# A recurrent attention layer with its gradients: order of the last forward block's stores, and one operand loaded in two halves

## The chip, the cores and the metric

The kernel runs on one core of a Trainium2 chip, as one program. Five engines work side by side, each through its own instructions in order: PE (TensorE, matrix products; its weight loads are listed apart as PEld), DVE (VectorE), ACT (ScalarE), POOL (GpSimd) and SP (SyncE, which here only issues DMAs). They wait for each other by semaphores. The metric is the device time of one execution in microseconds (us), median of several runs; lower is better.

## The reference

A sequence of 2048 rows of 512 numbers is normalised to `xn`. Output and all gradients are wanted of

```python
return x + _A_ref(xn, A_mem0, A_Wq, A_Wk, A_Wv, A_Wo, A_seg_len) + _B_ref(xn, B_w1, B_b1, B_w2, B_b2)
```

`_A_ref` goes through 64 segments of 32 rows, one after another. Each is attended together with 8 memory rows, 32 heads of 128, and the first 8 rows of its result are the next segment's memory:

```python
for s in range(n_seg):
    xs = x[:, s * seg_len:(s + 1) * seg_len, :].copy()
    h = jnp.concatenate([mem, xs], axis=1)
    q = jnp.einsum('btd,dhe->bhte', h, Wq)      # k, v alike
    ...
    p = _softmax(scores, axis=-1)
    o = jnp.einsum('bhqk,bhke->bhqe', p, v)
    o = jnp.einsum('bhte,hed->btd', o, Wo)
    mem = o[:, :M, :].copy()
    outs.append(o[:, M:, :])
```

`_B_ref` is a dense layer with bias, squared ReLU and a second dense layer (512 to 1792 to 512). `reference` calls `jax.vjp` and returns the output and ten gradients: of `x`, the first memory, Wq, Wk, Wv, Wo, w1, b1, w2, b2. The inputs are bf16.

## The kernel before

The work stands in five stages, in this order of time: the dense layer forward and backward (to about 240 us); the **forward chain** over 64 segments (to about 1125); the **left backward chain** (to about 1345); the backward chain over the segments, last to first; and the weight gradients as large products.

In the forward chain four segments make a block, 16 blocks in all. What depends only on the sequence itself, and not on the segment before, is the block's "left" part: the memory rows' own queries, keys and values. The order of all steps is written out by hand in the strings F_ORDER, one string for each of the four segments of a block. A name such as `q0mm+++` is a step of a segment, `L.lp` a step of a block's left part; each `+` delays it by one segment or block, and the strings are played for blocks 0 to 18, so that the last ones hold only what is left over. `play` calls each step once where its name stands.

Steps of a block's left part that the change touches, all of them DMAs on SP: `mtr` (L793) turns the memory rows' values vM into vTM, a tile with one buffer; `mst` (L794) stores it to S_VTM; `lp` (L844) stores the probabilities EL to S_PL; `otr` and `lo` (L841, L847) turn the left attention output OTL into ON and store it to S_OL; `lb` (L850) loads the dense result `bb`, to which DVE adds the block's output rows (L853). `t0` to `t3` and `u0` to `u3` turn and store the segments' attention output OT; for the last block, `t3` turns all four groups into one tile OCl and `u3` stores them (L782, L789), and then calls `st["late"]`, which is `otr` and `lo`. Other DMAs between them: `aw` and `as` (L946, L947) turn the dense layer's hidden gradients through a tile `box` to S_GH1N.

While the forward chain ends, PE also transposes the weights (ps_wt, copied back by ACT and DVE in turn), for the backward stages.

The left backward chain (`lback`, LB_ORDER) takes the 16 blocks in the order SEQ, beginning with 13, 14, 15. For each it needs the turned values l_vTL and l_vTM, the probabilities l_P and the keys l_kM and l_kL. The first block's loads, and the first dense chunk's, are issued by POOL (`first`), the later ones by SP (`ld`). Its PE work is interleaved with the dense weight gradients: each block carries one chunk of 256 hidden columns, `part` (wB, 1 MB, two buffers), against `side` (wA, 2 MB, all 2048 rows of the output gradient), written W0a, W0b, W1a, W1b. Blocks 1 to 7 make the gradient of w2 from `gflat` (each `a` half takes the first 8 of 16 row groups, each `b` half the others; L1106); blocks 9 to 15 make that of w1, with `side` loaded anew from S_XN (L1111). The chain's own stores (S_GOL, S_GSL, S_GQL) go out on POOL.

The tiles of the left backward chain lie in the SBUF space of the forward chain's tiles, so a first load waits until the last reader of what lay there is done, a DMA store among them. Names in the profile: tiles without buffer numbers, `S_...` for buffers in DRAM, `ps_...` for PSUM.

Of the kernel before, what the change touches and what calls it, by code (L numbers as in the profile page):

```python
# [10 lines left out]
BF16 = mybir.dt.bfloat16  # L11
F32 = mybir.dt.float32
P = 128
# [13 lines left out]
def kernel(  # L27
# [27 lines left out]
    nc = tc.nc  # L55

    _, S, D = A_x.shape
# [5 lines left out]
    L = M + SEG  # L63
# [3 lines left out]
    TC = S // P  # L67
# [21 lines left out]
    gflat = grad_out.flatten_outer_dims()  # L89
# [5 lines left out]
    dma = nc.sync.dma_start  # L95
    pdma = nc.gpsimd.dma_start
# [4 lines left out]
    NB = NSEG // SPB  # L101
# [12 lines left out]
    S_XN = dram.tile([S, D], BF16, name="S_XN")  # L114
# [6 lines left out]
    S_B = dram.tile([S, D], BF16, name="S_B")  # L121
# [9 lines left out]
    S_VTM = dram.tile([NB, P, KH, HG, NL], BF16, name="S_VTM")  # L131
    S_PL = dram.tile([NB, P, KH, KW], BF16, name="S_PL")
# [77 lines left out]
    with sb("p1b", 2) as p1b, sb("p1", 1) as p1:  # L210
# [90 lines left out]
        for rb in range(NRB):  # L301
# [5 lines left out]
            for fc in range(FC):  # L307
                ps = pst([P, RB], F32, name="ps_h1")
# [343 lines left out]
    def play(order, n, steps, lefts, step, blk, done=None):  # L652
# [37 lines left out]
        "tu1+++ w1+++ L.lq++ oa1+++ ob1+++ g0+++ g1+++ soN++ ra+++ rb+++ ta+++ Ha+++ tb+++ L.otr+ Hb+++ L.E3+ "  # L690
# [4 lines left out]
        "ta+++ Ha+++ rb+++ tb+++ Hb+++ km+++ L.t3+ q0mm++++ L.E5+ k0mm++++ L.ra+ xa+++ k0ev++++ q1mm++++ k1mm++++ "  # L695
# [5 lines left out]
    with psum("fr", 4) as fr, psum("fpp", 1) as fpp, \  # L701
# [58 lines left out]
        def left(b):  # L760
# [13 lines left out]
            for g in range(HG):  # L774
                def tO(g=g):
                    if b < NB - 1:
                        st["OC", g] = fo.tile([P, KH, P], BF16, name="OC", tag="OC", bufs=2)
                        nc.sync.dma_start_transpose(st["OC", g][:], B_["OT"][:, g].rearrange("p k j r -> p (k j r)"))
                    elif g == HG - 1:
                        st["OC"] = fs.tile([P, HG, KH, P], BF16, name="OCl", tag="OT")  # L780
                        for x in range(HG):
                            nc.sync.dma_start_transpose(st["OC"][:, x], B_["OT"][:, x].rearrange("p k j r -> p (k j r)"))  # L782

                def uO(g=g):
                    if b < NB - 1:
                        dma(S_ON[b, g], st["OC", g][:].rearrange("p k e -> p (k e)"))
                    elif g == HG - 1:
                        for x in range(HG):
                            dma(S_ON[b, x], st["OC"][:, x].rearrange("p k e -> p (k e)"))  # L789
                        st["late"]()  # L790
                o["t%d" % g], o["u%d" % g] = tO, uO

            o["mtr"] = lambda: nc.sync.dma_start_transpose(B_["vTM"][:].rearrange("p k g r -> p k (g r)"), B_["vM"][:])  # L793
            o["mst"] = lambda: dma(S_VTM[b], B_["vTM"][:])  # L794
            for p in range(2):
                def S_(p=p):
                    ps["s%d" % p] = big("ps_scL")
# [52 lines left out]
            o["lb"] = lambda: dma(B_["bb"][:], S_B[b * P:(b + 1) * P, :])  # L850

            def out():
                nc.vector.tensor_tensor(out=B_["bb"][:], in0=ps["B"][:], in1=B_["bb"][:], op=ALU.add)  # L853
# [140 lines left out]
    with sb("la", 2) as la, sb("ls", 2) as ls, sb("lo", 1) as lo_, sb("wg", 2) as wg, psum("lpp", 1) as lpp, psum("lr", 4) as lr:  # L994
# [8 lines left out]
        def lback(i_):  # L1003
# [10 lines left out]
            def load(i1, q=nc.sync):  # L1014
                T1, b1 = lb[i1][1], SEQ[i1]
                if i1:
                    turned_rows(T1["vTL"][:], b1, 2)
                q.dma_start(T1["vTM"][:], S_VTM[b1])
                q.dma_start(T1["P"][:], S_PL[b1])
                memory_rows(T1["kM"], b1, 2 * GW, q)  # L1020
                q.dma_start(T1["kL"][:], S_NL[b1][:, 1, :])

            def ld():
# [51 lines left out]
        NCH = F // CH  # L1075
        side, part = {}, {}

        def job(b):

            n, second = (b - 1, False) if b <= NCH else (b - NCH - 2, True)  # L1080
            return (n if 0 <= n < NCH else None), second

        def chunk(b, eng=dma):
            n, second = job(b)
            if n is None or b in part:
                return
            if n == 0:
                side[second] = wg.tile([P, TC, D], BF16, name="wA", tag="wA", bufs=1)
                pdma(side[second][:], (S_XN[:] if second else gflat).rearrange("(c p) f -> p c f", p=P))
            part[b] = wg.tile([P, TC, CH], BF16, name="wB", tag="wB")  # L1090
            eng(part[b][:], (S_GH1N if second else S_AN)[n])

# [4 lines left out]
        def product(b, i, x, ps):  # L1097
            n, second = job(b)
            if n is None:
                turns(2 if b == 0 else 5)  # L1100
                return
            if x == 0:
                ps["w", i] = big("ps_w")
            if not second:
                for rc in range(x * TC // 2, (x + 1) * TC // 2):
                    nc.tensor.matmul(ps["w", i][:], lhsT=part[b][:, rc, i * P:(i + 1) * P], rhs=side[False][:, rc, :],  # L1106
                                     start=(rc == 0), stop=(rc == TC - 1))
            else:
                dc = 2 * i + x
                for rc in range(TC):  # L1110
                    nc.tensor.matmul(ps["w", i][:, x * CH:(x + 1) * CH], lhsT=side[True][:, rc, dc * P:(dc + 1) * P],  # L1111
                                     rhs=part[b][:, rc, :], start=(rc == 0), stop=(rc == TC - 1), skip_group_check=True)
            if n == NCH - 1 and not second and i == 0 and x == 1:
                ps["b2"] = big("ps_gb2")
                for rc in range(TC):
                    nc.tensor.matmul(ps["b2"][0:1, :], lhsT=ones_col[:, :], rhs=side[False][:, rc, :], start=(rc == 0),
                                     stop=(rc == TC - 1))

        def keep(b, i, ps):
# [575 lines left out]
```

## Time and profile before

| | |
|---|---|
| median of 3 runs | 2846.58 us (2843.75 to 2865.32) |
| profiled execution | 2851.62 us, its span 2849.8 us |
| PE busy | 2660.2 us, 93% of the span |
| DVE, ACT, POOL busy | 1296.4, 976.6, 659.3 us |
| granted TensorE clock, mean | 0.979 |
| chain that ended last | PE 85%, issue 4%, DMA 4%, DVE 4%, SP's queue 2%, ACT 2% |
| DMA | 586.76 MB, mean 206 GB/s |

A row of the timeline reads: start in us from the span's start, busy us, engine, line, operation, result <- operands, form, number, and in brackets the idle time of that engine before it with what ended it. "SPq" is SP's DMA issuing; a DMA's row shows how long the issue took, not the transfer. A row of DMA issues ends with the median time from issue to landing. A row of waits says who waited for whom: us in total, times, longest. PE is the engine that sets the end almost everywhere, so a wait elsewhere counts only if PE comes to wait for it.

### The profile page before, as it was taken

How to read it: one execution, taken by the hardware profiler on the slowest of the kernel's cores; microseconds unless marked ns; L12 is line 12 of the kernel's file. 1: busy time of each engine (PE TensorE's matmuls, PEld its weight loads, DVE VectorE, ACT ScalarE, POOL GpSimd, SP SyncE). 2: the span in 40 equal slices, each digit the busy share in tenths (PEclk: the TensorE clock that was granted, in tenths of full speed). 3: DMA queues.
4: the chain of work that ended last, by engine and by line, in shares of the span. 5: the costliest groups of instructions: out<-in, count | busy, mean ns of one | idle time of the engine just before them, and what ended most of it. 6: DMA issues, size and time to landing. Idle time of an engine off the chain costs nothing.

```text
span 2849.8 us, 116970 instructions
## 1 busy us (share of the span) xinstructions
PE 2660.2 (93%) x52405; PEld 1452.3 (51%) x52405; DVE 1296.4 (45%) x3819; ACT 976.6 (34%) x2266; POOL 659.3 (23%) x1280
## 2 busy tenths in 40 slices
PE   7998999999999998888899899998999999999999
PEld 3444555555555556456455455555555544444444
DVE  4544656666666655344455555554555501100000
ACT  2323444444444445232333333333333301111111
POOL 1000000000000000123333433443334333322221
PEclk9999999999999999899999999999999999999999
DMA  9855689899989988998678877778777899999994
GB/s 248 273 193 179 162 190 216 214 214 220 219 208 220 222 207 184 268 244 229 157 186 175 205 189 175 181 198 205 175 178 192 236 337 199 210 221 206 212 205 84
DMA packets 840440, 586.76 MB, mean 206 GB/s; under 512 B 638001, under 2 KB 727746, under 8 KB 836610
## 3 DMA queue, kind: packets, MB, share of 16 engines
q1 hardware_dynamic: 798722, 455.76, 70.7%
q0 software_dynamic: 40928, 123.25, 14.9%
q8 instruction: 411, 6.73, 1.0%
q14 instruction: 91, 0.75, 0.1%
q10 hardware_dynamic: 288, 0.26, 0.0%
HBM read 184.95 MB, written 248.79 MB: 152 GB/s over the span
## 4 chain that ended last, share of the span: by engine, by line
PE 85%; issue 4%; DMA 4%; DVE 4%; SPq 2%; ACT 2%; POOL 0%; ACTq 0%; DVEq 0%; POOLq 0%
PE ps_gw L1653 19%; PE ps_proj L374 16%; PE ps_gR L492 12%; PE ps_R L492 5%; PE ps_RL L1260 3%; PE ps_tr L167 3%; PE b_pp L623 3%; PE ps_L L374 3%; PE ps_sc L464 2%; PE f_pp L623 2%; PE ps_B L345 2%; PE b_T L528 2%; PE ps_gxb L354 2%; PE f_T L528 2%; PE ps_w L1106 2%
## 5 line engine op out<-in xcount | busy, mean ns | idle before, releaser
L1653 PE MATMUL ps_gw<-gn,HNc 128*128 128x512 bf16 x1920 | 416.5, 379 | 0.0
L1653 PEld LDWEIGHTS <-HNc 128*128 128x128 bf16 x1920 | 187.9, 98 | 223.9
L419 ACT CAST f_N<-ps_proj 128x512 bf16<-128x512 f32 x320 | 184.0, 581 | 192.3 <-PE ps_proj L374 185.5
L1583 ACT CAST wt<-ps_gw 128x512 bf16<-128x512 f32 x128 | 73.7, 589 | 442.2 <-PE ps_gw L1653 410.4
L374 PEld LDWEIGHTS <-X 128*32 128x32 bf16 x5760 | 143.6, 96 | 134.0 <-DVE X L537 20.6
L1566 DVE TENSOR_TENSOR gx<-ps_rows,gb 128x512 f32<-128x512 f32 x16 | 11.1, 692 | 415.6 <-PE ps_rows L1564 415.6
L884 POOL COPY kM<-f_kT 128x256 bf16<-128x256 bf16 x64 | 25.8, 403 | 753.1 <-DVE f_kT L422 563.6
L492 PE MATMUL ps_gR<-Wv,gv 128*32 128x512 bf16 x2048 | 136.2, 390 | 6.0 <-issue 3.9
L1653 PE MATMUL ps_gw<-GOc,gn 128*128 128x512 bf16 x640 | 140.7, 382 | 1.2 <-DVE gm L1499 1.1
L492 PE MATMUL ps_R<-Wo,OT 128*32 128x256 bf16 x4096 | 131.6, 279 | 10.3 <-DMA Wo<-in_A_Wo_dram 4.5
L492 PE MATMUL ps_gR<-Wk,gk 128*32 128x512 bf16 (+1 forms) x2048 | 129.2, 375 | 3.6 <-issue 3.5
L374 PE MATMUL ps_proj<-Wo,GT 128*32 128x512 bf16 x2048 | 124.3, 384 | 5.7 <-DVE GT L1305 5.1
L1584 POOL DMA_DIRECT2D out_dram<-wt x120 | 65.0, 543 | 277.4 <-ACT wt L1583 260.5
L419 ACT CAST gON<-ps_proj 128x512 bf16<-128x512 f32 x128 | 75.0, 586 | 157.8 <-PE ps_proj L374 157.8
L374 PE MATMUL ps_proj<-Wq,X 128*32 128x512 bf16 x1920 | 126.0, 380 | 0.1
L492 PE MATMUL ps_gR<-Wq,gq 128*32 128x512 bf16 (+1 forms) x2048 | 120.3, 354 | 5.6 <-issue 5.6
L374 PE MATMUL ps_proj<-Wk,X 128*32 128x512 bf16 x1920 | 123.7, 382 | 0.6
L374 PE MATMUL ps_proj<-Wv,X 128*32 128x512 bf16 x1920 | 121.9, 378 | 0.2 <-issue 0.2
L1341 POOL COPY PD<-b_P 32x320 bf16<-32x320 bf16 x256 | 115.1, 450 | 14.9 <-DMA b_P<-S_A 3.7
L492 PEld LDWEIGHTS <-OT 128*32 128x32 bf16 x4096 | 105.6, 98 | 20.5 <-issue 13.5
L419 ACT CAST gk<-b_pp 128x256 bf16<-128x256 f32 x128 | 48.1, 376 | 166.6 <-PE b_pp L623 163.3
L492 PEld LDWEIGHTS <-gq 128*32 128x32 bf16 x2816 | 75.0, 98 | 56.2 <-issue 20.4
(291 smaller groups left out, 5278.8 us busy)
## 6 DMA issues: line engine op xcount, KB each, us to landing
S_A<-f_N SPq DMA_DIRECT2D x64, 512.0 KB
out_dram<-wt POOLq DMA_DIRECT2D x134, 128.0 KB, 5.5
S_A<-f_N SPq DMA_DIRECT2D x64, 256.0 KB
S_GB<-gv SPq DMA_DIRECT2D x32, 512.0 KB
S_GB<-gk SPq DMA_DIRECT2D x32, 512.0 KB
S_GB<-gq SPq DMA_DIRECT2D x32, 512.0 KB
b_qN<-S_A POOLq DMA_DIRECT2D x63, 256.0 KB, 4.3
b_kN<-S_A POOLq DMA_DIRECT2D x63, 256.0 KB, 5.2
```

Of the source, the lines that this page charges most:

```text
L167: nc.tensor.transpose(ps_ap, in_ap, ident[base:base + k, base:base + k])
L345: nc.tensor.matmul(psB[:], lhsT=aT[:, fc, rc * P:(rc + 1) * P], rhs=W2[:, fc, :], start=(fc == 0), stop=(fc == FC - 1))
L374: nc.tensor.matmul(o, lhsT=hT[:, dc, :], rhs=x, start=(dc == 0), stop=(dc == DC - 1), tile_position=(0, 32 * g))
L419: nc.scalar.copy(out, in_)
L492: nc.tensor.matmul(R[32 * g:32 * g + 32, 0:(cs.stop - cs.start) * P].rearrange("p (a b) -> p a b", b=P), lhsT=XT(k, g), rhs=x[:, cs, :], s ...
L528: nc.tensor.transpose(st["T", h][:, 0, c * P:(c + 1) * P], st["R4"][:, (2 * h + c) * P:(2 * h + c + 1) * P], identF[:])
L623: nc.tensor.matmul(o, lhsT=N_[32 * g:32 * g + m, kk * P:(kk + 1) * P], rhs=X(kk)[32 * g:32 * g + m], start=(i == 0), stop=(i == len(jobs) ...
L1260: nc.tensor.matmul(ps["R", i][32 * g:32 * g + 32, :].rearrange("p (a b) -> p a b", b=P), lhsT=B_[n][:, k, g, :], rhs=W(g * KH + k), start= ...
L1341: nc.gpsimd.tensor_copy(PD[32 * g:32 * g + 32, g], C["P"][32 * g:32 * g + 32, :, KW - L:KW])
L1583: nc.scalar.copy(wt[:], ps[:])
L1584: eng(dst, wt[:])
L1653: nc.tensor.matmul(ps[:], lhsT=l(rc), rhs=r(rc), start=(n == 0), stop=(n == RC_ALL - 1))
```

## The change

Three things. First, for the last block alone (`end = "z"`), the steps `mtr`, `lp`, `mst` and `lb` get names of their own, `mtrz`, `lpz`, `mstz` and `lbz`, which stand one or two strings earlier in F_ORDER than their plain names. Second, `otr` and `lo` of the last block are made where they are made for the others, and `late` goes. Third, `side` is two tiles of 8 row groups each, with a load for each; for the output gradient both are issued by POOL ahead of the first block's l_kL rather than behind it.

```diff
-        "k1ev+++ L.tu1+ q0fl+++ kl+++ xb++ L.mst k1fl+++ as- k0Te+++ soV++ q1ev+++ q0Te+++ L.W1+ q1fl+++ k1Te+++ "
-        "q1Te+++ L.hs+ L.oa1+ s0+++ mx0+++ sb0+++ L.X0+ v0mm+++ soP++ L.ob1+ s1+++ ex0+++ v1mm+++ su0+++ mx1+++ "
+        "k1ev+++ L.tu1+ q0fl+++ kl+++ xb++ L.mst L.mtrz+ k1fl+++ as- k0Te+++ soV++ q1ev+++ q0Te+++ L.W1+ L.lpz+ q1fl+++ k1Te+++ "
+        "q1Te+++ L.hs+ L.oa1+ s0+++ mx0+++ sb0+++ L.X0+ L.mstz+ v0mm+++ soP++ L.ob1+ s1+++ ex0+++ v1mm+++ su0+++ mx1+++ "
...
-        "kl+++ q0fl+++ as- xa++ q1ev+++ k0Te+++ k1fl+++ q1fl+++ q0Te+++ s0+++ L.ldL++ k1Te+++ mx0+++ q1Te+++ sb0+++ "
+        "kl+++ q0fl+++ as- xa++ L.lbz+ q1ev+++ k0Te+++ k1fl+++ q1fl+++ q0Te+++ s0+++ L.ldL++ k1Te+++ mx0+++ q1Te+++ sb0+++ "
...
-                        st["late"]()
...
+            end = "z" if b == NB - 1 else ""
+            o["mtr" + end] = lambda: nc.sync.dma_start_transpose(B_["vTM"][:].rearrange("p k g r -> p k (g r)"), B_["vM"][:])
+            o["mst" + end] = lambda: dma(S_VTM[b], B_["vTM"][:])
...
-            o["otr"] = otr if b < NB - 1 else lambda: None
+            o["otr"] = otr
-            o["lp"] = lambda: dma(S_PL[b], B_["EL"][:])
+            o["lp" + end] = lambda: dma(S_PL[b], B_["EL"][:])
-            o["lo"] = lo if b < NB - 1 else lambda: None
-            st["late"] = lambda: (otr(), lo())
-            o["lb"] = lambda: dma(B_["bb"][:], S_B[b * P:(b + 1) * P, :])
+            o["lo"] = lo
+            o["lb" + end] = lambda: dma(B_["bb"][:], S_B[b * P:(b + 1) * P, :])
...
                 memory_rows(T1["kM"], b1, 2 * GW, q)
+                if i1 == 0:
+                    half_side(False, 0)
+                    half_side(False, 1)
                 q.dma_start(T1["kL"][:], S_NL[b1][:, 1, :])
...
+        TH = TC // 2
+        def half_side(second, h, eng=pdma):
+            side[second, h] = wg.tile([P, TH, D], BF16, name="wA", tag="wA%d" % h, bufs=1)
+            eng(side[second, h][:], (S_XN[:] if second else gflat)[h * TH * P:(h + 1) * TH * P, :].rearrange(
+                "(c p) f -> p c f", p=P))
+        def side_rows(second, rc):
+            return side[second, rc // TH][:, rc % TH, :]
...
-            if n == 0:
-                side[second] = wg.tile([P, TC, D], BF16, name="wA", tag="wA", bufs=1)
-                pdma(side[second][:], (S_XN[:] if second else gflat).rearrange("(c p) f -> p c f", p=P))
+            if n == 0 and second:
+                half_side(True, 0)
+                half_side(True, 1)
...
-                    nc.tensor.matmul(ps[...], lhsT=part[b][:, rc, i * P:(i + 1) * P], rhs=side[False][:, rc, :],
+                    nc.tensor.matmul(ps[...], lhsT=part[b][:, rc, i * P:(i + 1) * P], rhs=side_rows(False, rc),
```

The instructions of PE, ACT and DVE and their order are the same in both. On SP, from the last segment's turn of `box` on to the first load of the next chain, the order before is (a row is line, operation, result <- operand, shape):

```order
L794 DMA S_VTM<-vTM 128x1024
L947 DMA S_GH1N<-box 128x1024
L864 DMA S_HT<-X 512x1x128
L946 DMA_TRANSPOSE box<-S_GH1T 128x4x256
L857 DMA out_dram<-bb 128x512
L947 DMA S_GH1N<-box 128x1024
L946 DMA_TRANSPOSE box<-S_GH1T 128x4x256
L782 DMA_TRANSPOSE OCl<-OT 128x8x128 x4
L947 DMA S_GH1N<-box 128x1024
L850 DMA bb<-S_B 128x512
L789 DMA S_ON<-OCl 128x1024 x4
L841 DMA_TRANSPOSE ON<-OTL 128x8x128
```

After these come L847 S_OL, L793 vTM, L844 S_PL, the first l_vTL and l_vTM, and only then L794 S_VTM. After the change the same stretch of SP's queue is:

```order
L794 DMA S_VTM<-vTM 128x1024
L793 DMA_TRANSPOSE vTM<-vM 128x8x128
L946 DMA S_GH1N<-box 128x1024
L844 DMA S_PL<-EL 128x512
L863 DMA S_HT<-X 512x1x128
L794 DMA S_VTM<-vTM 128x1024
L945 DMA_TRANSPOSE box<-S_GH1T 128x4x256
L841 DMA_TRANSPOSE ON<-OTL 128x8x128
L856 DMA out_dram<-bb 128x512
L946 DMA S_GH1N<-box 128x1024
L849 DMA bb<-S_B 128x512
L847 DMA S_OL<-ON 128x1024
```

The last box turn, the four OCl turns, S_GH1N, the four S_ON stores and the output store follow, and then l_vTL. So the last block's vTM, S_PL, S_VTM, ON, bb and S_OL stand ahead of OCl, and one line number less marks the same step below L787.

On POOL, at the beginning of the left backward chain, before (gol is the gradient at the memory rows):

```order
L1002 DMA gol<-S_GLT 128x2048
L1018 DMA l_vTM<-S_VTM 128x1024
L1019 DMA l_P<-S_PL 128x512
L637 DMA l_kM<-S_A 32x1x1024 x4
L1021 DMA l_kL<-S_NL 128x1024
L1089 DMA wA<-in_grad_out_dram 128x16x512
L1091 DMA wB<-S_AN 128x4096
```

and after:

```order
L1001 DMA gol<-S_GLT 128x2048
L1017 DMA l_vTM<-S_VTM 128x1024
L1018 DMA l_P<-S_PL 128x512
L637 DMA l_kM<-S_A 32x1x1024 x4
L1084 DMA wA<-in_grad_out_dram 128x8x512 x2
L1023 DMA l_kL<-S_NL 128x1024
L1103 DMA wB<-S_AN 128x4096
```

The two halves stand ahead of l_kL. The second operand, wA from S_XN, is likewise two issues in place of one, at the same place of POOL's queue.

More of the change, by code (lines that the diff above doesn't have):

```diff
@@ L789, in uO @@
                             dma(S_ON[b, x], st["OC"][:, x].rearrange("p k e -> p (k e)"))
-                        st["late"]()
                 o["t%d" % g], o["u%d" % g] = tO, uO
-            o["mtr"] = lambda: nc.sync.dma_start_transpose(B_["vTM"][:].rearrange("p k g r -> p k (g r)"), B_["vM"][:])
-            o["mst"] = lambda: dma(S_VTM[b], B_["vTM"][:])
+            end = "z" if b == NB - 1 else ""
+            o["mtr" + end] = lambda: nc.sync.dma_start_transpose(B_["vTM"][:].rearrange("p k g r -> p k (g r)"), B_["vM"][:])
+            o["mst" + end] = lambda: dma(S_VTM[b], B_["vTM"][:])
             for p in range(2):
@@ L1105, in product @@
                 for rc in range(x * TC // 2, (x + 1) * TC // 2):
-                    nc.tensor.matmul(ps["w", i][:], lhsT=part[b][:, rc, i * P:(i + 1) * P], rhs=side[False][:, rc, :],
+                    nc.tensor.matmul(ps["w", i][:], lhsT=part[b][:, rc, i * P:(i + 1) * P], rhs=side_rows(False, rc),
                                      start=(rc == 0), stop=(rc == TC - 1))
@@ L1110, in product @@
                 for rc in range(TC):
-                    nc.tensor.matmul(ps["w", i][:, x * CH:(x + 1) * CH], lhsT=side[True][:, rc, dc * P:(dc + 1) * P],
+                    nc.tensor.matmul(ps["w", i][:, x * CH:(x + 1) * CH], lhsT=side_rows(True, rc)[:, dc * P:(dc + 1) * P],
                                      rhs=part[b][:, rc, :], start=(rc == 0), stop=(rc == TC - 1), skip_group_check=True)
@@ L1115, in product @@
                 for rc in range(TC):
-                    nc.tensor.matmul(ps["b2"][0:1, :], lhsT=ones_col[:, :], rhs=side[False][:, rc, :], start=(rc == 0),
+                    nc.tensor.matmul(ps["b2"][0:1, :], lhsT=ones_col[:, :], rhs=side_rows(False, rc), start=(rc == 0),
                                      stop=(rc == TC - 1))
```

## The prediction

> **What bounds the kernel now.** I read the page first: PE is busy 93% of the span and the chain that ended last is 85% PE, so only a stretch in which PE stands still can give much back. The change touches one such stretch, the handover from the forward chain to the left backward chain near 1100 to 1175 us, and the dense products' second operand near 1240. PE's waits in the first, longest first (us in total, times, longest):
>
> ```profile
> PE ps_w L1106 <- DMA wB<-S_AN: 7.7, 2, 7.1
> PE l_pp L623 <- issue: 5.4, 1, 5.4
> PE ps_wt L167 <- DVE Wq L422: 2.8, 1, 2.8
> ```
>
> Three stalls, 15.3 us without the short second wait for wB. Next, who released whom, from the chain in order of time (start, us), and the POOL queue's instructions there:
>
> ```profile
> 1132.77 19.24 DMA S_PL<-EL
> ...
> 1152.59 0.52 POOL wB L1091
> ```
> ```profile
> 1130.15 0.58 POOL L1021 DMA_DIRECT2D l_kL<-S_NL  x1 [26.82 <-DVE Wq L422]
> 1130.80 1.19 POOL L1089 DMA_DIRECT2D wA<-in_grad_out_dram  x1
> 1152.58 0.55 POOL L1091 DMA_DIRECT2D wB<-S_AN  x1 [20.59 <-ACT l_gq L419]
> ```
>
> POOL issues in order. The chain shows what its second wait was for: the store of the last block's probabilities EL (S_PL), 19.24 us under way, because wB's buffer takes over the space where EL lay. Its first wait, 26.82 us ahead of l_kL, is put down to DVE, but the program's own waits name the four stores of OCl to S_ON: l_kL takes that space. wA, 2 MB, stood behind it. Last, how full the DMA engines were (columns: stretch, length, busy of PE, PEld, DVE, ACT, POOL, then granted clock, DMA share, GB/s):
>
> ```profile
> 1108.00:1118.00 10.00, 9.79 (x170) 7.88 (x168) 4.93 (x9) 6.80 (x7) 0.00 (x0) 0.88 0.32 86
> 1130.00:1145.00 15.00, 12.36 (x260) 8.61 (x258) 7.86 (x17) 8.44 (x12) 1.78 (x2) 0.84 1.11 121
> 1236.00:1242.00 6.00, 6.00 (x106) 3.17 (x99) 0.40 (x2) 2.94 (x7) 0.58 (x1) 1.00 0.11 33
> ```
>
> Ten microseconds nearly empty (share 0.32), then fifteen over full, at 121 GB/s: the wA load, the vTM turn, S_PL and the turned l_vTL all at once. The change moves work from the second stretch into the first.
>
> **The change part by part.** Sync's queue, before (start, us, issue):
>
> ```profile
> 1099.98 0.42 SPq L794 DMA_DIRECT2D S_VTM<-vTM  x1
> 1108.61 1.25 SPq L946 DMA_TRANSPOSE box<-S_GH1T  x1
> 1115.77 1.23 SPq L946 DMA_TRANSPOSE box<-S_GH1T  x1
> 1117.09 6.14 SPq L782 DMA_TRANSPOSE OCl<-OT  x4
> 1123.90 0.43 SPq L850 DMA_DIRECT2D bb<-S_B  x1
> 1124.37 2.01 SPq L789 DMA_DIRECT2D S_ON<-OCl  x4
> 1133.51 11.85 SPq L632 DMA_TRANSPOSE l_vTL<-S_NL  x1
> ```
> ```profile
> SPq L947 <- DMA box<-S_GH1T: 6.2, 2, 3.5
> SPq L946 <- DMA S_GH1N<-box: 5.8, 2, 3.7
> SPq L794 <- DMA vTM<-vM: 4.9, 1, 4.9
> ```
>
> The moved vTM turn must wait until the previous block's S_VTM has left the single vTM buffer, and everything on SP waits behind it. With 3.7 us for a 256 KB store after its issue, that is 1099.98 + 0.42 + 3.7 = 1104.1. From there I walk the new order with the waits just quoted: vTM turn to 1105.6; S_GH1N and, once DVE has written EL, S_PL to about 1107.4; S_HT to 1108; S_VTM 4.9 after the turn, 1110.5; box turn to 1112.2 (before 1109.9); ON turn to 1113.4; S_GH1N 3.5 after the box, 1115.7; bb at 1116.2, S_OL, the last box turn 3.7 after S_GH1N, 1119.8 (before 1115.77); the four OCl turns to 1127.2; the four S_ON stores to about 1130. So bb comes 7.7 us sooner, S_PL 25 us sooner, and the S_ON stores about 3.5 us later. PE does not wait for SP between 1100 and 1122 (no such row above), so the walk itself costs nothing; the price is term 4.
>
> *Term 1, the bb load.* DVE stands at the last output sum until bb is there; Wq's copies queue behind it on DVE, and PE behind them (the rows after it are PE's, for this and the next terms):
>
> ```profile
> 1127.03 0.69 DVE L853 TENSOR_TENSOR bb<-ps_rows,bb 128x512 bf16<-128x512 f32 x1 [3.97 <-DMA bb<-S_B]
> ```
> ```profile
> 1123.08 2.47 PE L167 MATMUL ps_wt<-ident,Wq 128*128 128x128 bf16 x38
> 1128.37 4.43 PE L167 MATMUL ps_wt<-ident,Wq 128*128 128x128 bf16 x40 [2.82 <-DVE Wq L422]
> 1141.27 0.20 PE L623 MATMUL l_pp<-l_gST,l_kM 32*128 32x32 bf16 x4
> 1149.72 1.89 PE L167 MATMUL ps_wt<-ident,Wv 128*128 128x128 bf16 x16
> 1159.57 3.60 PE L1106 MATMUL ps_w<-wA,wB 128*128 128x512 bf16 x8 [7.11 <-DMA wB<-S_AN]
> 1163.73 2.54 PE L1106 MATMUL ps_w<-wA,wB 128*128 128x512 bf16 x8
> 1168.35 1.90 PE L1106 MATMUL ps_w<-wA,wB 128*128 128x512 bf16 x8
> 1173.40 1.90 PE L1106 MATMUL ps_w<-wA,wB 128*128 128x512 bf16 x8 [0.57 <-DMA wB<-S_AN]
> ```
>
> The 2.82 us go, since DVE wanted bb at 1127.03 - 3.97 = 1123.06, and a load issued at 1116.2 is there by then. The 40 transposes after it ran at the lowered clock: 38 took 2.47 us, so 40 take 2.6, not 4.43. Together -4.6, between -2.8 (idle alone) and -4.6. The Trainium skill, "TensorE: Matmul & The Clock Gate", section "What's actually happening", says the clock falls to half after an idle window of about 3.4 us; a gap of 2.8 us need not lower it, and by that page this term would be -2.8 and the sum 1.8 smaller. The trace has 40 transposes at 0.11 us each behind that very gap, so I follow the trace.
>
> *Term 2, the 5.4 us "issue" stall* in the over-full stretch. What PE awaited is not shown; instructions come by the same DMA engines. With less traffic it should shrink, not surely vanish: the backward chain has such stalls of up to 3.7 us in a normal load:
>
> ```profile
> PE b_pp L623 <- issue: 39.4, 33, 3.7
> ```
>
> Bounds 0 and -5.4; I take half, -2.7. The 16 transposes behind it (1.89 us; 1.04 at 2.47 for 38) give another -0.85.
>
> *Term 3, wB.* The load waits now only for the vTM turn, long done, and for its place behind l_kL. l_kL leaves when the S_ON stores have landed: 1130.15 before, 3.5 us later now, 1133.7; wB 0.6 later, 1134.3. Their landing times, KB and us:
>
> ```profile
> wA<-in_grad_out_dram POOLq DMA_DIRECT2D x1, 2048.0 KB, 21.2
> wB<-S_AN POOLq DMA_DIRECT2D x1, 1024.0 KB, 6.9
> ```
>
> wB lands at 1141.2. PE now comes to its first product at 1159.57 - 7.11 = 1152.46; with terms 1 and 2 gone (8.15), at 1144.3. The 7.1 us go whole.
>
> *Term 4, l_kL.* PE wants it (with l_kM) for the first l_pp, at 1141.27 - 4.6 = 1136.7. Given wB's 6.9 us it lands at 1140.6: a new wait of +3.9, between 0 (if it lands as the wait ends) and +12 (second rival). Everything of the left chain queues behind it on PE.
>
> *Term 5, the cold start of the products.* 3.60 and 2.54 us for eight against 1.90, and 0.57 for the next wB: -2.9; 0 if term 4's wait should leave PE as cold as now.
>
> *Term 6, the second operand at 1240.* Here the load of 2 MB (wA from S_XN) stands ahead of the chain's own stores in POOL's queue:
>
> ```profile
> PE l_pp L623 <- ACT l_gq L419: 9.9, 1, 9.9
> ```
> ```profile
> 1237.08 1.90 PE L1106 MATMUL ps_w<-wA,wB 128*128 128x512 bf16 x8
> ```
> ```profile
> 1241.42 1.17 POOL L1089 DMA_DIRECT2D wA<-S_XN  x1 [12.04 <-PE ps_tr L167]
> 1242.58 0.55 POOL L1068 DMA_DIRECT2D S_GOL<-l_gON  x1
> ```
> ```profile
> 1259.32 1.07 ACT L419 CAST l_gON<-ps_proj 128x512 bf16<-128x512 f32 x2 [10.32 <-DMA S_GOL<-l_gON]
> S_GOL<-l_gON POOLq DMA_DIRECT2D x3, 256.0 KB, 16.2
> ```
>
> PE's 9.9 us are ACT's 10.3 us, and those are S_GOL's, which drains behind wA. The halves still stand ahead of S_GOL, but the first is free when the product over its rows ends, 1238.98, not 1241.42, and the DMA engines are idle then (share 0.11). So the same bytes start 2.4 us sooner: -2.0, between 0 and -2.4. Against it, the Trainium skill, "DMA: Bandwidth & Descriptors", section "Anatomy of one DMA — SWDGE (gpsimd) path", gives each POOL-issued DMA a fixed 2.0 us besides its bytes; a second half would cost 2 us, and by that page this term would be 0 and the sum 2.0 smaller. Its formula, an estimate of 6.8 us for 2 MB, is far under the 21.2 us of the row above: here queueing sets the time, not a fixed part.
>
> Two more DMA issues on POOL (1.17 us whole for 2 MB) cost nothing: POOL stood 26.82 us in front of l_kL.
>
> Sum: -4.6 - 2.7 - 0.85 - 7.1 + 3.9 - 2.9 - 2.0 = -16.3 us. The profiled execution took 2851.6 (span 2849.8 and 1.8 around it), which gives 2835.3; it lay 5.0 over the median of the runs, 2846.6, so against that I say **2830**.
>
> **The rivals.** *Less, by contention.* The first half waits for S_HT (X's space), so goes at about 1108 + 3.7 = 1111.7. The second waits for PE's turns of the last block's left sums, which end at 1117.6:
>
> ```profile
> 1116.93 0.66 PE L545 MATMUL ps_sum<-identF,R4L 128*128 128x128 f32 x4 [0.21 <-ACT Wo L419]
> ```
>
> It then runs beside the OCl turns. In the over-full stretch a turn beside wA took 11.85 us to issue, and 1 MB of it is a half of the load. If OCl and S_ON lose 8 us, l_kL and wB land near 1149: term 4 becomes +12, term 3 stays, since wB follows l_kL closely, term 5 falls to 0: sum -5, 2841. For it: share 1.06 to 1.11 whenever turns and a large load meet. Against: the first MB goes into the ten nearly idle microseconds.
>
> *More.* The issue stall goes whole (-5.4), l_kL is in time (0), and the halves take away 9.9 us at 1240, because the bytes that S_GOL waits for have been halved when it is issued: -4.6 - 5.4 - 0.85 - 7.1 - 2.9 - 9.9 = -31, 2816. Against: S_GOL is still behind both halves.
>
> *Slower.* The left keys and wB are now behind 2 MB on a queue that drains in order, and the S_ON stores that l_kL waits for come 3.5 us later. If the second half starts only when wA did, at 1130.8, and takes the same 21.2 us, it lands at 1152; wB, which before was issued just then and landed 6.9 us later, cannot land before 1159, and with SP's later turns beside it 3.5 us after that, 1162.4. PE's first product starts 3 us later than now and as cold; with term 6 at 0 that is +3, 2850. It decides if the second half leaves after about 1128; its waits end at 1117.6.
>
> That the change does not do what it says, because wA's space comes free late anyway, is this case without the 3.5 us.
>
> **How the numbers follow.** Forecast 0.55, less by contention 0.22, more 0.15, slower 0.08. The range leaves out a part of "more" and the far end of "slower": 2814 to 2848. A measurement of this kernel tells about 1%, 28 us, from no change: faster by over that needs nearly all of "more" plus the forecast's lower tail, 0.21; slower by over that only something not named here, 0.05; within it 0.74.
>
> **What would show it.** In the new profile: bb's sum on DVE without its 3.97 us; PE's wait for wB gone and wB issued near 1134; the first wA half near 1112 and the second near 1118; a wait of a few us for l_kL at the first l_pp; eight products in 1.9 us from the start; near 1240 ACT's wait for S_GOL at about 8 us. I am wrong if l_kL is issued after 1140, if PE's issue stall grows, or if wB's landing comes after PE.

## The result, and the profile after

The changed kernel takes **2837.57 us** (median of 20 runs, 2832.44 to 2849.46); the kernel before, on the same chip beside it, 2846.57 us (20 runs, 2836.67 to 2865.32). The ratio is **0.9961, 95% interval 0.9947 to 0.9975**: 11 us less, between 7 and 15 (the two medians are 9.0 apart). The forecast was 2830 with a range of 2814 to 2848. The profiled execution of the changed kernel took 2843.92 us (span 2841.8).

DVE's instructions are the same in number and order in both programs, so the same instruction can be looked up in both traces. I call **handover** the time from DVE's reduction of the last block's left sums into XT to the subtraction that opens the left chain's softmax gradient behind the second operand's load. Its two ends in the timeline of the kernel before:

```profile
1120.38 0.87 DVE L552 TENSOR_REDUCE XT<-ps_sum 128x32 f32<-128x128 f32 x4
...
1267.12 0.42 DVE L572 TENSOR_TENSOR ds_t<-ps_sc,l_P 128x256 f32<-128x256 f32 x1 [3.32 <-PE ps_sc L464]
```

and in that of the changed kernel:

```profile
1122.21 0.87 DVE L552 TENSOR_REDUCE XT<-ps_sum 128x32 f32<-128x128 f32 x4
...
1252.57 0.42 DVE L572 TENSOR_TENSOR ds_t<-ps_sc,l_P 128x256 f32<-128x256 f32 x1 [3.24 <-PE ps_sc L464]
```

146.74 us before and 130.36 after: 16.4 less in this pair, next to a forecast of 16.3. That agreement is an accident, as the experiments show. PE's waits in that stretch, changed kernel (us in total, times, longest):

```profile
PE l_pp L623 <- ACT l_gq L419: 4.4, 2, 3.9
PE l_pp L623 <- DMA l_kL<-S_NL: 3.0, 1, 3.0
PE ps_wt L167 <- DVE Wq L422: 2.7, 1, 2.7
...
PE ps_w L1118 <- DMA wB<-S_AN: 1.8, 1, 1.8
```

The wait of 7.1 us for the first wB and the issue stall of 5.4 are gone; a new one of 3.0 for the left keys l_kL stands there, as forecast. But PE still waits 2.7 us behind Wq's copies. POOL's queue and then SP's, changed kernel, in order of time:

```profile
1113.78 0.94 POOL L1084 DMA_DIRECT2D wA<-in_grad_out_dram  x1 [7.75 <-DVE Wk L422]
1119.98 0.91 POOL L1084 DMA_DIRECT2D wA<-in_grad_out_dram  x1 [5.27 <-PE ps_wt L167]
1139.98 0.56 POOL L1023 DMA_DIRECT2D l_kL<-S_NL  x1 [19.09 <-DMA out_dram<-bb]
1140.54 0.55 POOL L1103 DMA_DIRECT2D wB<-S_AN  x1
```
```profile
1106.45 1.25 SPq L793 DMA_TRANSPOSE vTM<-vM  x1
...
1115.66 0.61 SPq L856 DMA_DIRECT2D out_dram<-bb  x1
...
1122.57 0.32 SPq L849 DMA_DIRECT2D bb<-S_B  x1
...
1126.59 7.04 SPq L782 DMA_TRANSPOSE OCl<-OT  x4
...
1134.35 1.89 SPq L789 DMA_DIRECT2D S_ON<-OCl  x4
```

The halves leave at 1113.8 and 1120.0 (forecast 1112 and 1118). SP is 2.3 us behind the forecast walk at the vTM turn and comes to the load of bb near 1117.1, where the walk has 1116.2; there, behind the previous block's output store of 1115.66, it stands until 1122.57. Its longest waits there:

```profile
SPq L849 <- DMA out_dram<-bb: 5.5, 1, 5.5
SPq L793 <- DMA S_VTM<-vTM: 3.7, 1, 3.7
```

The tile bb has one buffer, so the last block's load into it cannot leave before the previous block's sum has been stored out of it, and that store was under way beside the first half of the operand. DVE and PE behind it:

```profile
1128.75 0.69 DVE L852 TENSOR_TENSOR bb<-ps_rows,bb 128x512 bf16<-128x512 f32 x1 [3.86 <-DMA bb<-S_B]
```
```profile
1130.09 2.39 PE L167 MATMUL ps_wt<-ident,Wq 128*128 128x128 bf16 x40 [2.71 <-DVE Wq L422]
...
1149.22 2.06 PE L1118 MATMUL ps_w<-wA,wB 128*128 128x512 bf16 x8
...
1162.54 1.90 PE L1118 MATMUL ps_w<-wA,wB 128*128 128x512 bf16 x8 [1.82 <-DMA wB<-S_AN]
```

DVE waits 3.86 us for bb, where it waited 3.97. How full the DMA engines were (columns as before: clock, DMA share, GB/s at the end):

```profile
1108.00:1118.00 10.00, 10.00 (x172) 8.25 (x171) 5.83 (x11) 6.90 (x10) 0.94 (x1) 0.83 1.02 191
...
1130.00:1145.00 15.00, 11.18 (x253) 8.32 (x253) 8.49 (x18) 7.04 (x10) 2.19 (x4) 0.92 0.93 247
```

The ten idle microseconds are full now (share 1.02, was 0.32). And the second operand, POOL's queue and ACT's wait behind it:

```profile
1229.64 0.91 POOL L1084 DMA_DIRECT2D wA<-S_XN  x1 [9.90 <-PE ps_w L1118]
1231.77 0.90 POOL L1084 DMA_DIRECT2D wA<-S_XN  x1 [1.23 <-PE ps_tr L167]
```
```profile
1244.84 1.07 ACT L419 CAST l_gON<-ps_proj 128x512 bf16<-128x512 f32 x2 [5.49 <-DMA S_GOL<-l_gON]
```

The first half leaves 2.1 us before the second; ACT's wait is 5.49 us, not 10.32.

### The profile page after: what moved, and what is told of

It is laid out like the page before. It is cut to its first block, busy times and chain, and to the rows that moved or that the text cites. A ratio compares the mean times of both kernels' runs of the same rounds, so it can differ in the third digit from the quotient of the medians.

```text
span 2841.8 us, 116977 instructions
## 1 busy us (share of the span) xinstructions
PE 2657.2 (94%) x52405; PEld 1451.6 (51%) x52405; DVE 1297.4 (46%) x3819; ACT 976.6 (34%) x2266; POOL 661.0 (23%) x1282
## 4 chain that ended last, share of the span: by engine, by line
PE 47%; issue 3%; DVE 1%; ACT 0%; DMA 0%; POOL 0%; ACTq 0%; POOLq 0%; DVEq 0%; SPq 0%
PE ps_gw L1665 19%; PE ps_gR L492 12%; PE ps_proj L374 4%; PE ps_RL L1272 3%; PE b_pp L623 3%; PE b_T L528 2%; PE ps_tr L167 1%; PE ps_sc L464 1%; PE b_pp L1405 1%; PE ps_R L492 1%; DVE gOT L422 1%; ACT R L419 0%; PE b_pp L1407 0%; PE ps_rows L1576 0%; DVE ds_t L572 0%
```

## The experiments

All results in one table: the handover of each profiled execution, the longest waits of PE in it (for Wq behind bb; for l_kL; for wB at a product; behind ACT's wait for S_GOL), and the ratio to the kernel before on the same chip, where it was timed.

| kernel | handover, us | bb | l_kL | wB | S_GOL | ratio (95%) |
|---|---|---|---|---|---|---|
| before | 146.7 | 2.8 | - | 7.1 | 9.9 | |
| before_again | 139.9 | 3.2 | - | 7.9 | 7.5 | |
| before_third | 137.5 | 2.0 | - | 8.2 | 7.6 | |
| after | 130.4 | 2.7 | 3.0 | 1.8 | 3.9 | 0.9961 (0.9947 to 0.9975) |
| after_again | 132.6 | 3.7 | 1.7 | 1.3 | 4.5 | 0.9960 (0.9936 to 0.9985) |
| halves_only | 134.4 | 8.7 | - | 1.3 | 4.6 | 0.9975 (0.9956 to 0.9994) |
| moves_only | 139.4 | - | 1.4 | 13.7 | 7.6 | 0.9993 (0.9971 to 1.0014) |
| second_late | 133.9 | 3.1 | 3.6 | 1.4 | 8.3 | 0.9974 (0.9954 to 0.9993) |
| bb_own | 134.7 | 2.1 | 2.3 | 1.2 | 3.8 | 0.9970 (0.9949 to 0.9991) |
| split | 138.6 | 3.7 | 3.0 | 6.0 | 4.6 | 0.9981 (0.9957 to 1.0005) |
| half1_sp | 132.8 | 3.7 | 5.1 | 0.9 | 4.4 | 0.9983 (0.9960 to 1.0006) |
| vtm_early | 129.9 | 1.8 | 3.2 | 1.8 | 3.4 | 0.9985 (0.9964 to 1.0005) |
| vtm_bb | 134.2 | - | 0.9 | 4.4 | 3.9 | 1.0009 (0.9982 to 1.0036) |
| vtm_half1 | 127.6 | - | 5.4 | 0.7 | 4.7 | 0.9992 (0.9973 to 1.0010) |

**The same kernels again.** No edit: a second and a third profile of the kernel before, and the changed kernel a second time.

> The kernel before once more, for a second profile. The five profiles of changed kernels all lose 4 to 17 us against the first profile of before between 1345 us and the start of the dense part, where all programs are the same. If that first profile only ran that stretch unusually fast (chance in which executions stall), this one is slower there by 3 to 10 us, and the change's own gain is the 16 us of the handover less nothing. If the change itself costs the later stretch something, this one runs it as the first did, within 2 us.

> The kernel before, a third profile. If the 5.4 us stall of PE without a shown cause ahead of the first l_pp is a matter of chance, as the second profile (1.2 us) suggests, this one has under 2.5 us there; if the first profile showed the rule, 4 us or more. From 1120 to 1272 us: between 0 and -8 against the first profile; the wait for the first wB 6 to 9 us, the one behind S_GOL 7 to 10 us.

> The changed kernel once more. Handover (1120 to 1270 us) again -14 to -17 against before if its terms are fixed by the program; the stretch from 1345 us on differs by 3 us or more from the first profile if it varies by chance. Median 9 us under before.

PE's waits in the second profile of the kernel before, and its 40 transposes:

```profile
PE ps_w L1106 <- DMA wB<-S_AN: 10.3, 3, 7.9
PE l_pp L623 <- ACT l_gq L419: 8.4, 2, 7.5
...
PE l_pp L623 <- issue: 1.2, 1, 1.2
```
```profile
1131.59 2.39 PE L167 MATMUL ps_wt<-ident,Wq 128*128 128x128 bf16 x40 [3.18 <-DVE Wq L422]
```

the same transposes in the second profile of the changed kernel, behind a longer gap:

```profile
1129.61 3.25 PE L167 MATMUL ps_wt<-ident,Wq 128*128 128x128 bf16 x40 [3.70 <-DVE Wq L422]
```

and the waits in the third profile of the kernel before:

```profile
PE ps_w L1106 <- DMA wB<-S_AN: 10.2, 2, 8.2
PE l_pp L623 <- ACT l_gq L419: 8.5, 2, 7.6
...
PE l_pp L623 <- issue: 1.2, 2, 0.7
```

The issue stall of 5.4 us and the 4.43 us for 40 transposes belong to the first profiled execution alone; the waits for wB and behind S_GOL come back every time. The handover is 146.7, 139.9 and 137.5 us before, 130.4 and 132.6 after: means of 141.4 and 131.5, **9.9 us apart**, next to 9 to 11 in the timed runs. From the handover's end to one of DVE's sums gx near 2400, where the last large products begin and up to which the program is the same, the three executions of before took 1133, 1147 and 1129 us, the two of the changed kernel 1140 and 1124. So the 6 us by which the first changed profile fell back there lie within what executions of one program differ by, no cost of the change is seen there, and a single pair of profiles can be off by as much as the change is worth. Three of the numbers expected above were missed: the second profile of before is 14 us slower in that stretch, not 3 to 10; the change's own gain is not the 16 us of the first pair; and the third's handover is 9 us shorter than the first's, not 0 to 8.

**One part of the change alone.** Each diff from here on is against the changed kernel. `halves_only` leaves SP's order as it was:

```diff
-  ... L.mst L.mtrz+ ... L.W1+ L.lpz+ ... L.X0+ L.mstz+ ... xa++ L.lbz+ ...
+  ... L.mst ... L.W1+ ... L.X0+ ... xa++ ...
-            end = "z" if b == NB - 1 else ""
+            end = ""
...
-            o["otr"] = otr
+            o["otr"] = otr if b < NB - 1 else lambda: None
-            o["lo"] = lo
+            o["lo"] = lo if b < NB - 1 else lambda: None
+            st["late"] = lambda: (otr(), lo())
```

> The operand in two halves ahead of the left keys, Sync's order as before the change (vTM turn, S_PL, ON turn and S_OL behind OCl). If the gain comes from taking the 2 MB load out of the crowded stretch, wB still waits for S_PL but S_PL lands fast: issue stall of 5.4 us gone, wait for the first wB 2 to 5 us in place of 7.1, wait at the second operand 3.9 as in the changed kernel; from 1120 to 1270 us about -11, median about 2838. If the gain comes from Sync's moves (S_PL sooner), wB's wait stays at 7 us or grows and the stretch gives under -6, median 2842 or more.

`moves_only` leaves the operand whole and behind the left keys:

```diff
-                if i1 == 0:
-                    half_side(False, 0)
-                    half_side(False, 1)
                 q.dma_start(T1["kL"][:], S_NL[b1][:, 1, :])
...
-            if n == 0 and second:
-                half_side(True, 0)
-                half_side(True, 1)
+            if n == 0:
+                side[second] = wg.tile([P, TC, D], BF16, name="wA", tag="wA", bufs=1)
+                pdma(side[second][:], (S_XN[:] if second else gflat).rearrange("(c p) f -> p c f", p=P))
```

> Sync's moves alone, the operand whole and behind the left keys as before the change. If the halves carry the gain: the whole load leaves near 1132 to 1135 and lands near 1154, PE waits 5 to 9 us for it at its first product, the wait at the second operand is 9.9 again; 1120 to 1270 us about -4, median 2843 or more. If the moves carry it: first product without a wait over 3 us, stretch -9 or better. bb's load: with no wA load beside the output's store it leaves by 1118, so DVE's wait for bb is gone; if it still leaves near 1122, the store's landing is not slowed by the operand's halves.

SP's rows in `halves_only`, and PE's longest wait:

```profile
1124.60 9.24 SPq L782 DMA_TRANSPOSE OCl<-OT  x4
...
1134.52 0.43 SPq L851 DMA_DIRECT2D bb<-S_B  x1
```
```profile
PE ps_wt L167 <- DVE Wq L422: 8.7, 1, 8.7
```

SP's rows, DVE's sum and PE's waits in `moves_only`:

```profile
1112.70 0.62 SPq L856 DMA_DIRECT2D out_dram<-bb  x1
...
1115.03 0.32 SPq L849 DMA_DIRECT2D bb<-S_B  x1
...
1118.97 5.37 SPq L782 DMA_TRANSPOSE OCl<-OT  x4
```
```profile
1121.71 0.69 DVE L852 TENSOR_TENSOR bb<-ps_rows,bb 128x512 bf16<-128x512 f32 x1 [0.22 <-PE ps_rows L564]
```
```profile
PE ps_w L1105 <- DMA wB<-S_AN: 13.7, 1, 13.7
...
PE l_pp L623 <- DMA l_kL<-S_NL: 1.4, 1, 1.4
```

Each part makes good what it promises and opens a hole that the other fills. With the halves alone, bb's load stands behind four OCl turns of 9.24 us (6.1 to 6.7 in the three profiles of before, without the second half beside them), and PE waits 8.7 us, which the theory did not have; still the stretch is 134.4 us, 7 under the mean of before. With the moves alone, bb leaves 2.3 us after the output store, DVE waits no more, l_kL is all but in time, and wB, behind the whole operand, then costs 13.7 us at the first product, more than the 5 to 9 expected: 139.4, 2 under before. The ratios (0.9975 and 0.9993) go the same way. So the halves seem to carry most of the gain; with one profile each and intervals that overlap, the shares are not settled. And the store of bb that held SP for 5.5 us in the changed kernel is slow with the first half beside it: SP waits 0.9 us for it in `moves_only`, and 4.1 to 6.2 us in the seven profiles that have both that half and this wait.

**The second operand.** `second_late` issues its halves in the other order, so that both wait for the last reader:

```diff
-                half_side(True, 0)
                 half_side(True, 1)
+                half_side(True, 0)
```

> The changed kernel with the two halves of the second operand issued in the opposite order, so that both start when the last product over the first operand has read it, as the whole load did. Theory (the early start of one half is what shortens the wait near 1240): ACT's wait for S_GOL and PE's behind it return to 8 to 10 us from 3.9, about +5 against the changed kernel, median 2842. Rival (two loads in place of one on POOL's queue let S_GOL's store through sooner, whenever they start): the wait stays at 4 to 5 us, same time as the changed kernel.

POOL's issue of both halves and ACT's wait:

```profile
1232.52 1.79 POOL L1084 DMA_DIRECT2D wA<-S_XN  x2 [12.04 <-PE ps_tr L167]
```
```profile
1249.07 1.07 ACT L419 CAST l_gON<-ps_proj 128x512 bf16<-128x512 f32 x2 [8.98 <-DMA S_GOL<-l_gON]
```

The wait is back at 8.98 us: what shortens it is that half of the bytes start 2.1 us sooner, not that there are two loads. That was this theory, and PE's 8.3 in place of 3.9 to 4.5 agrees. Why 2.1 us of head start bring 3.5 us on ACT and 3.8 to 4.4 on PE stays open.

**Taking the wait for bb away.** `bb_own` gives the last block but one another buffer for its sum:

```diff
                     pool, shape, dt = shapes[n]
+                    if n == "bb" and b == NB - 2:
+                        return fo.tile(shape, dt, name=n, tag="wtt")
                     return pool.tile(shape, dt, name=n, tag=n)
```

> The changed kernel with another buffer for the block-sum tile bb of the last block but one, so that the last block's bb load needs not wait for the store of the block before. Theory (the step that failed is a buffer wait that stands in front of Sync's queue): bb leaves near 1117 in place of 1122.6, DVE's wait of 3.9 us and PE's of 2.7 us go, OCl and S_ON come about 5 us sooner and the wait of 3.0 us for l_kL shrinks to 0 to 1: about -5 against the changed kernel, median 2832 to 2834. Rival (the DMA engines, not the buffer, set it): the OCl turns run beside the second half and take as much longer, l_kL is issued no sooner than 1138, and only PE's 2.7 us move into the l_kL wait: 0 against the changed kernel, 2837.

SP's rows, and ACT's longest wait (a cast in the left chain whose tile lies where the forward chain's OT lay):

```profile
1116.78 0.81 SPq L858 DMA_DIRECT2D out_dram<-bb  x1
...
1119.61 0.43 SPq L851 DMA_DIRECT2D bb<-S_B  x1
...
1126.24 10.04 SPq L784 DMA_TRANSPOSE OCl<-OT  x4
```
```profile
ACT l_gOT L419 <- DMA OCl<-OT: 6.6, 1, 6.6
```

bb's load now leaves 2.8 us after the output store, not 6.9. But it runs beside the halves, and DVE still waits for it (PE 2.1 us); the OCl turns take 10.04 us, l_kL leaves at 1142.5, and ACT is held by the turns: PE waits 5.9 us for l_gOT. 134.7 us: no gain, the rival's case. But the vTM turn also waited 8.2 us here, 4.5 more than in the changed kernel, so this run alone does not settle it; the next runs show what that wait goes with.

**The second half behind the turns.** `split` puts it behind l_kL and wB; `half1_sp` lets SP issue it behind the output store:

```diff
                 if i1 == 0:
                     half_side(False, 0)
-                    half_side(False, 1)
...
-            o["first"] = lambda: (load(i_, nc.gpsimd), chunk(i_ + 1, pdma))
+            o["first"] = lambda: (load(i_, nc.gpsimd), chunk(i_ + 1, pdma), half_side(False, 1))
```
```diff
                 if i1 == 0:
                     half_side(False, 0)
-                    half_side(False, 1)
+                    half_side(False, 1, dma)
```

> The changed kernel with the first half of the operand ahead of the left keys as before, but the second half behind the left keys and wB. Theory (the second half beside the OCl turns is what holds Sync's queue: four turns took 5.4 us without it and 7.0 to 10.0 beside it, and bb's load 6 us): bb leaves near 1115, DVE has no wait for it, l_kL leaves near 1132 and PE has no wait over 1.5 us for it; the second half lands 14 to 18 us later, so PE waits 2 to 6 us at the second half of its first product: 3 to 6 us less than the changed kernel up to 1200. Rival (the bytes have to pass anyway before the first product ends): what is saved comes back as a wait of 8 us or more at the product, 0 or slower against the changed kernel.

> The changed kernel with the second half of the operand issued by Sync, behind the S_ON and output stores and ahead of the turn of l_vTL, near 1128 to 1131. By the theory of the split run: OCl turns in 5.4 us, no wait for bb, l_kL near 1132 with a wait under 2 us, the second half there by 1142 and wB by 1146, so that PE waits 0 to 3 us at the product: 4 to 8 us less than the changed kernel up to 1200. Rival: l_kL and wB, beside that half, land 5 us later each, and the wait moves to l_pp and the product: no gain.

POOL's and SP's rows in the changed kernel and then in `split`, and SP's longest wait in `split`:

```profile
1101.66 0.42 SPq L794 DMA_DIRECT2D S_VTM<-vTM  x1
```
```profile
1101.69 0.57 POOL L1001 DMA_DIRECT2D gol<-S_GLT  x1 [14.23 <-DMA vM<-S_A]
```
```profile
1102.15 0.56 POOL L1001 DMA_DIRECT2D gol<-S_GLT  x1 [13.33 <-DMA vM<-S_A]
```
```profile
1103.15 0.42 SPq L794 DMA_DIRECT2D S_VTM<-vTM  x1
```
```profile
SPq L793 <- DMA S_VTM<-vTM: 8.7, 1, 8.7
```

Both missed, for a reason that neither theory had: the vTM turn, at the head of the moved steps, waited 8.7 and 8.9 us for the store S_VTM (3.7 in the changed kernel), and everything on SP came as much later: OCl turns in 6.1 and 6.5 us, but l_kL at 1142. The wait goes with the order of two issues on different queues, the store on SP and POOL's load of gol (512 KB). Where gol left 0.8 to 1.0 us ahead (bb_own, half1_sp, split), SP waited 8.2, 8.9 and 8.7 us; where 0.3 ahead (moves_only), 5.4; where within 0.2 us of it (after, after_again, second_late), 3.6 to 3.8. That the order is the cause is not shown: no run moves it alone, and POOL's loads of l_vTM and l_P follow gol within 1.4 us.

The two runs still tell what each half does to bb, since only the first is near it there. SP waits 5.1 and 4.7 us for the store, as in the changed kernel; but from the issue of bb's load to DVE's sum it takes 2.1 and 2.2 us, where the five profiles in which a half is on its way beside that load have 3.8 to 7.0. So DVE's wait in the changed kernel has two parts: the store beside the first half, the load beside the second.

**S_VTM sooner.** `vtm_early` moves that store for every block; `vtm_bb` does so on top of `bb_own`, `vtm_half1` on top of `half1_sp`:

```diff
-        "q0fl+++ xb++ L.u1 k0fl+++ ...
+        "q0fl+++ xb++ L.u1 L.mst k0fl+++ ...
...
-        "k1ev+++ L.tu1+ q0fl+++ kl+++ xb++ L.mst L.mtrz+ ...
+        "k1ev+++ L.tu1+ q0fl+++ kl+++ xb++ L.mtrz+ ...
```

> The changed kernel with every block's S_VTM store one place in the order sooner (some 6 to 8 us), so that in the last block it has landed before the vTM turn wants the buffer, whatever the load of gol does. Theory (the wait of 3.7 to 9 us at the head of Sync's queue holds all behind it, and its length hangs on whether gol's load gets ahead of that store): the vTM turn starts within 1.5 us of the vM loads' landing, about 2 to 3 us sooner against the forward chain than in the changed kernel; bb's load still waits for the output store, so DVE's wait shrinks by 0 to 2 us only: 0 to -3 up to 1200. Rival: Sync waits at the next row in its place and nothing moves.

> The changed kernel with both waits at the head of Sync's queue taken away: S_VTM sooner, and another buffer for the block-sum tile of the last block but one. Theory: bb leaves by 1116 and DVE has no wait for it, PE's 2.7 to 3.7 us go; OCl turns from 1120, beside the second half, 7 to 10 us; l_kL leaves at 1134 to 1137 and its wait is under 2 us: 4 to 7 us less than the changed kernel up to 1200, median about 2837 where the changed kernel gives 2843. Rival (the second half and the turns share the DMA engines): OCl turns 10 us or more, l_kL at 1139 as now, no gain.

> The changed kernel with S_VTM sooner and the second half of the operand issued by Sync behind the output store, so that neither the head of Sync's queue nor that half stands beside the OCl turns. Theory (what the change still loses is the second half beside the turns and the wait at the vTM turn): OCl turns under 6.5 us, l_kL issued 3 to 5 us sooner against the last output sum than in the changed kernel, PE's waits for Wq and l_kL together 1 to 4 us where the changed kernel has 5.4 to 6.7 and wB's under 3: 2 to 5 us less than the changed kernel from 1120 to 1272 us, that is -16 to -20 against the first profile of before. Rival (the bytes set it): wB and l_kL share the engines with that half and land as late, the sum of those waits stays at 6 us or more and the stretch at -13 to -15.

PE's waits in `vtm_bb`, and DVE's sum and PE's wait in `vtm_half1`:

```profile
PE ps_w L1120 <- DMA wB<-S_AN: 4.4, 1, 4.4
PE ps_sc L464 <- ACT l_gOT L419: 3.5, 1, 3.5
```
```profile
1134.82 0.69 DVE L852 TENSOR_TENSOR bb<-ps_rows,bb 128x512 bf16<-128x512 f32 x1 [0.22 <-PE ps_rows L564]
```
```profile
PE l_pp L623 <- DMA l_kL<-S_NL: 5.4, 1, 5.4
```

`vtm_early` came out as its theory said: the vTM turn no longer waits for S_VTM and starts 2.4 to 2.9 us sooner against the handover's beginning, PE's wait for bb is 1.8 us, the handover 129.9. In the other two the wait for bb is gone, and comes back one place on: at l_gOT and wB behind 9.9 us of turns in `vtm_bb`, at l_kL in `vtm_half1`. The handover of the latter, 127.6, is the shortest of all and as its theory had it, while the sum of its waits for Wq, l_kL and wB, 6.1 us, is the rival's. None of the three is faster in whole: where the handover begins, `vtm_bb` and `vtm_half1` are at 1134.5 and 1131.9 us, all others between 1118.8 and 1125.1. `vtm_early` began at 1124.1, yet the timed ratios of all three (0.9985, 1.0009, 0.9992) lie above both of the changed kernel (0.9961, 0.9960). That points to a cost of the sooner store in the forward chain, where every block has it; what it is was not looked for, and it is not shown. No version was found that beats the changed kernel.

## Why the prediction was right, and where not

The sum had six terms. Beside each forecast stands the first pair of profiles, and then the mean of the two changed profiles against the mean of the second and third of before, the two without the stalls that terms 1 and 2 priced:

| term | forecast | first pair | the others |
|---|---|---|---|
| 1, wait for bb | -2.8 | -0.1 | +0.6 |
| 1, the 40 transposes | -1.8 | -2.0 | +0.4 |
| 2, issue stall | -2.7 | -5.4 | about 0 |
| 2, the 16 transposes | -0.85 | 0 | +0.8 |
| 3, first wB | -7.1 | -7.1 | -8.0 |
| 4, new wait for l_kL | +3.9 | +3.0 | +2.4 |
| 5, products and next wB | -2.9 | -0.9 | -1.4 |
| 6, second operand | -2.0 | -6.0 | -3.4 |
| sum | -16.3 | -18.5 | -8.6 |

The handover itself shrank by 16.4 in the first pair and by 7.2 against the second and third of before; small stalls that no term names are the rest.

- **Term 1 failed as a mechanism.** The step was "a load issued at 1116.2 is there by then". SP came to that load at about 1117.1, close to the walk, and could not issue it until 1122.57: the load writes the one buffer that the previous block's store was still reading. That store stands two rows ahead of the load in SP's new order, and the walk passes over it. I counted for every moved step what stood ahead of it on SP's queue, and for vTM also the store that must leave its buffer; for bb I did not ask that question. `moves_only`, where SP waits 0.9 us for that store, has DVE's wait gone; with the halves beside them, store and load are slow.
- **Terms 1 and 2 priced an accident.** The slow transposes and the issue stall occurred in one of three profiles of the kernel before. I held against the Trainium skill that 40 transposes were slow behind a gap of 2.82 us. The Trainium skill, "TensorE: Matmul & The Clock Gate", section "What's actually happening", lets the clock fall after an idle window of about 3.4 us. Ten of the eleven profiles that have this gap side with it: six gaps of 1.85 to 3.18 us were followed by 40 transposes in 2.39 us, four of 3.68 to 8.67 us by 40 in 3.25 to 4.00. The bound is not sharp, though: behind the wait for l_kL 16 transposes took 1.89 us after 3.00 us (after) and 1.07 us after 2.98 (split). One row was too little to set a rule aside; what slowed that one case is not shown.
- **Term 3 was right** and is most of the change's gain: 7.1 to 8.2 us at the first wB in every profile of before, none in the two after. `moves_only` says why: without the halves ahead of the keys it is 13.7. wB left at 1140.5, not 1134.3, and took 8.4 us, not 6.9, so it was there only 0.3 us before PE started its first product at 1149.2, where the forecast had 1144.3 plus 3.9. The forecast's margin of 7 us was gone; that the wait went whole all the same is partly luck.
- **Term 4** was right in kind; that it is near in size (3.0 and 1.7) is luck. In the first changed profile l_kL left at 1139.98, 6.3 us behind the walk, most of it SP's 5.5 us at bb; it landed in 3.3 us, not in the 6.9 taken over from wB; and PE came to it at 1140.4, not 1136.7, with the wait for bb still ahead of it.
- **Term 5** was about half as large as forecast: in after_again the products still start cold.
- **Term 6** was mis-sized: 3.4, not 2.0, from the same cause (`second_late`). By the fixed 2.0 us that the Trainium skill, "DMA: Bandwidth & Descriptors", section "Anatomy of one DMA — SWDGE (gpsimd) path", gives each such load, a second load should have eaten it, as the prediction estimated. No run shows a loss of that size: with both halves late ACT waits 8.98 us (`second_late`), with the whole load 8.24 to 8.55 in three profiles and 10.32 in the first.

So the forecast of 2830 lay 7.6 us too low, the range held, and the result is within 1%, as the likeliest of the three outcomes said. Of the rivals, "less, by contention" was right that the halves would hold up SP's queue, but looked for it in the wrong place. The OCl turns took 7.04 and 6.55 us, against 6.1 to 6.7 before; the time went at the store of bb, beside the half that the prediction sent into "the ten nearly idle microseconds" (SP waits 5.5 and 6.2 us). Its share of 1.06 is that of 1118 to 1130, where no large load runs beside the turns. l_kL left at 1140, and it did not come to a wait of 12. "Slower" asked that the second half leave after 1128; it left at 1120.

## What to carry to other kernels

Before moving a load forward, look up not only the queue that it joins but the last reader of the buffer that it writes, and which other transfer you are about to put beside that reader. Where a term of a sum is a stall or a slow row without a cause in the trace, take a second profile before pricing it: here such rows were 5 us of the 16 forecast. And a wait removed at a handover with full DMA engines may come back at the next consumer: with the wait for bb gone, `vtm_bb` waits 3.5 us at l_gOT and 4.4 at wB, `vtm_half1` 5.4 at l_kL, and neither is faster in whole.

## What the hardware showed that was not expected

Some 5 us go with the order of two transfers on different queues, issued at most a microsecond apart: the 256 KB store S_VTM held SP 3.6 to 3.8 us when it left within 0.2 us of POOL's 512 KB load, and 8.2 to 8.9 us when it left 0.8 to 1.0 us behind it; why is not shown. The length of the four OCl turns goes with how long the second half of the operand is still under way beside them (its issue plus its landing time): 5.4 to 6.7 us where it is not (seven profiles), 6.6 to 8.0 where it is for 1 to 2.5 us (four), 9.2 to 10.0 where for 6 to 7 us (`halves_only`, `bb_own`, `vtm_bb`). And executions of the same program differ by up to 18 us in one stretch of some 1130 us (1129 to 1147 for the kernel before, 1124 to 1140 for the changed one), so that this change can be seen in the medians and in its own stretch, but not in the span of one profile.
